# Moving two casts of q and k, and one batch's transposes, in the queues of a fused attention and mixer kernel

## The chip, the cores and the metric

The kernel runs on one core of a Trainium2 chip. A core has five engines that work side by side and keep in step through semaphores: TensorE (PE in the profile; its weight loads are PEld), VectorE (DVE), ScalarE (ACT), GpSimd (POOL) and SyncE (SP). Each takes its instructions in the order in which the program wrote them for that engine. Transfers between the chip's memory (DRAM here) and the on-chip buffers are issued by an engine and carried out by 16 DMA engines; this kernel issues them from SP and from POOL, and each of these two has its own DMA queue. An instruction that waits holds up everything behind it on its engine, a DMA that is to be issued too.

The metric is the time of one execution on the device in microseconds (us), the median of several runs.

## The reference

Eight batches, 8 heads, 576 tokens, head dimension 64. Attention with a causal mask and a bias made from a running sum of s; then a mixer on the attention's output with a low-rank product over the tokens and a two-layer product over the channels:

```python
scores = scale * np.matmul(q, k.transpose(0, 1, 3, 2))
cum = np.cumsum(np.maximum(s, 0.0), axis=-1)
bias = -(cum[:, :, :, None] - cum[:, :, None, :])
scores = np.where(causal, -1000000000.0, scores + np.minimum(bias, 0.0))
attn = softmax(scores)                      # exp(scores - max), divided by its sum
x = (attn @ v) with the heads side by side  # (8, 576, 512)
h = xt @ U @ V                              # xt: x with tokens last; U 576x32, V 32x576
u = x + h.transpose(0, 2, 1)
out = u + np.maximum(u @ w_ch1, 0.0) @ w_ch2   # 512 -> 2048 -> 512
```

Inputs and output are float32; the products run in bfloat16.

## The kernel before

**Groups.** The mixer works on pairs of batches, four groups of 1152 tokens. While TensorE runs the two layers of one group (`layer1`, line 551; `layer2`, line 570), the attention of the next two batches is mixed into the same instruction streams. The function `beside` does that: it takes both as generators whose steps name a cost, and decides by these costs which of the two writes its next instructions. [...]

**Attention of a batch** (`attention`, `scores`, `weigh`). For each head: four rounds of score products on TensorE (line 323), an exponential on ACT behind each (line 329), and behind the second exponential a causal select on POOL (line 344), which puts zeros above the diagonal. The head is weighed with v (line 373) one head later, between the second and the third round of the next head; the last head of a batch is weighed right behind its own scores. After each head, `attention` calls `at_head(h)`, where the program puts transfers and conversions for later batches.

**How q and k come in.** From batch 3 on, `cast(b)` (line 153) issues two DMAs from POOL that read k and q of a batch as float32 and write them as bfloat16 into the DRAM scratch `kq_rows`. `turn_batch(b)` (line 766) then issues from SP, for each of the batch's four pairs of heads, two transposing DMAs from `kq_rows` into kT and qT (`turn_kq`, line 174) and two small transfers of bias rows (`bias_rows`, line 281) that have to follow them: 16 DMAs. kT and qT have room for two batches. Batch 2 comes in otherwise, through `load_six` on POOL's queue and transposes on TensorE; only its bias rows are transfers of SP.

**How v comes in.** `fetch_v(b, t)` (line 194) is a DMA from SP of 128 tokens (the fifth tile has 64) as float32 into the buffer vf, which holds one batch. `cast_v(b, t)` (line 200) converts a tile on POOL into v_raw, from which `weigh` reads it. A fetch for batch b+1 has to wait for the conversions of batch b.

**The stretch around the change**, in the order of the program:

- `second()`: the weighing of batch 1's last heads beside the first layers; then on POOL two kinds of memset on v_raw (lines 806, 808), the five cast_v(2, t), and cast(3). SP has just issued the five fetch_v(2, t) and the bias rows of batch 2.
- between the two calls of `beside`: on SP an output transfer, the five fetch_v(3, t), then turn_batch(3).
- the attention of batch 2 (c == 2 in `ahead_of`): behind head 5 cast_v(3, 0); behind head 6 cast(4), then cast_v(3, 1) and cast_v(3, 2); behind head 7 cast_v(3, 3), cast_v(3, 4), and on SP fetch_v(4, t).
- the attention of batch 3: behind head 0 turn_batch(4) on SP.
- `mix(1)`: on DVE the sum of x and the low-rank part (line 522), on SP the transposes of x into uT (line 526), which `layer1` of the second group reads.

Of the kernel before, what the change touches and what calls it, by code (L numbers as in the profile page):

```python
# [41 lines left out]
def kernel(  # L42
# [110 lines left out]
    def cast(b):  # L153
        for i, src in enumerate((k, q)):
            nc.gpsimd.dma_start(
                out=kq[i, HP * b : HP * b + HP, :PAIR].rearrange("n (r c) -> r n c", r=128),
                in_=src[b]
                .rearrange("(n h) s d -> n (h s d)", h=2)
                .rearrange("n (r c) -> r n c", r=128),
            )  # L160
# [8 lines left out]
    def turn_kq(n):  # L169
        if not n < BH // 2:  # L170
            return
        for i, to in enumerate((kT, qT)):
            rows = kq[i, n]
            nc.sync.dma_start(
                out=to[n % RING][:, : 2 * S],
                in_=bass.AP(
                    tensor=rows.tensor, offset=rows.offset, ap=[[D, 2 * S], [1, 2 * D]]
                ),
                transpose=True,
            )  # L180
# [11 lines left out]
    def fetch_v(b, t):  # L192
        rows = slice(128 * t, min(128 * t + 128, S))
        nc.sync.dma_start(
            out=vf0[v_rows(t), t], in_=v[b, :, rows].rearrange("h p d -> p h d")
        )

    def cast_v(b, t, engine=None):
        n = v_rows(t)
        (engine or nc.gpsimd).tensor_copy(v_raw[b // 2 % 2][n, 5 * (b % 2) + t, :, :D], vf0[n, t])  # L200
# [76 lines left out]
    def bias_rows(n):  # L277
        if not n < BH // 2:
            return
        for to, r in ((kT, A_K), (qT, A_Q)):  # L280
            nc.sync.dma_start(out=to[n % RING][D:KA, : 2 * S], in_=aug_v[r, n])
# [79 lines left out]
    def weigh(b, h, p, scalar=False):  # L361
        bi = b % 2
        vr, x = v_raw[b // 2 % 2], x_sb[b // 2 % 2]
        diag = (D0, D1, D2, D3, D4)
        off = (O0, O1, O2, O3)
        pv = bank("pv", 2)
        pv3 = pv[:, : 5 * (D + 1)].rearrange("p (t e) -> p t e", e=D + 1)
        for it in range(5):
            for j in range(it + 1):
                at = diag[j] if j == it else off[j] + 128 * (it - j - 1)  # L370
                if it == 4 and bi == 1:
                    at -= 64
                nc.tensor.matmul(  # L373
                    pv3[:, it, :], lhsT=p[:, at : at + 128],
                    rhs=vr[:, 5 * bi + j, h, :],
                    start=(j == 0), stop=(j == it),
                )
        rec = work.tile([128, 5], FP32, tag="rec", name="rec")
        nc.vector.reciprocal(rec, pv3[:, :, D])  # L379
        n = 5 if bi == 0 else 4  # L380
        if scalar:
            for t in range(n):
                nc.scalar.mul(x[:, t, h * D : h * D + D], pv3[:, t, :D], rec[:, t : t + 1])
            return
        nc.vector.tensor_mul(  # L385
            x[:, 5 * bi : 5 * bi + n, h * D : h * D + D], pv3[:, :n, :D],
            rec[:, :n].unsqueeze(2).to_broadcast([128, n, D]),
        )
        if bi:
            (nc.scalar.mul if b == 1 and h < H - 1 else nc.vector.tensor_scalar_mul)(  # L390
                x[64:128, TAIL, h * D : h * D + D], pv3[64:128, 4, :D], rec[64:128, 4:5]
            )
# [149 lines left out]
    def layer1(cuts, by_block=False):  # L542
        jobs = [(c, nf) for c in cuts for nf in range(16)]
        if by_block:

            jobs.sort(key=lambda job: job[1] + 1.5 * (job[0] != cuts[0]))
        for (c0, c1), nf in jobs:
            cw = c1 - c0
            f1 = bank("f", 3)
            for kt in range(4):  # L550
                nc.tensor.matmul(  # L551
                    f1[:, :cw], lhsT=w1[:, kt, 128 * nf : 128 * nf + 128],
                    rhs=uT[:, kt, c0:c1],
                    start=(kt == 0), stop=(kt == 3),
                )
                if kt == 1:
                    yield 2 * cw / 2400.0
            nc.scalar.activation(hT[:, nf, c0:c1], f1[:, :cw], RELU)  # L558
            yield 2 * cw / 2400.0

    def layer2(g, tl):
        for t in tl:
            more = g == 0 and t < TAIL

            last = g == len(GROUPS) - 1 and t == 8
            for cs in (slice(0, 256), slice(256, 512)) if last else (slice(0, 512),):
                cw = cs.stop - cs.start
                f2 = bank("f", 3)
                for kt in range(16):
                    nc.tensor.matmul(  # L570
                        f2[:, :cw], lhsT=hT[:, kt, 128 * t : 128 * t + 128], rhs=w2[:, kt, cs],
                        start=(kt == 0), stop=(kt == 15 and not more),
                    )
                    if kt % 2 == 1:
                        yield 0.43
                if more:
                    nc.tensor.matmul(
                        f2, lhsT=V_cat[:, t, :], rhs=ux0, start=False, stop=True
                    )
                o = work.tile([128, d_model], FP32, tag="o", name="o", bufs=5)  # L580
                nc.vector.tensor_add(o[:, :cw], x_sb[g % 2][:, t, cs], f2[:, :cw])  # L581
                if t == TAIL:
                    for bi, b in enumerate(GROUPS[g]):
                        nc.sync.dma_start(
                            out=out[b, 512:576, :], in_=o[64 * bi : 64 * bi + 64, :]
                        )
                else:
                    r0 = 128 * (t if t < TAIL else t - 5)
                    nc.sync.dma_start(
                        out=out[GROUPS[g][t > TAIL], r0 : r0 + 128, cs], in_=o[:, :cw]  # L590
                    )
# [3 lines left out]
    def beside(back, ahead, ratio, lead):  # L595
        due, live = -lead * ratio, True
        for cost in back:
            due += cost * ratio
            while live and due > 0:
                spent = next(ahead, None)  # L600
                if spent is None:
                    live = False
                else:
                    due -= spent
        for _ in ahead:
            pass
# [159 lines left out]
    def turn_batch(b, p0=0, p1=HP):  # L766
        for n in range(HP * b + p0, HP * b + p1):
            turn_kq(n)
            if n > HP * b:
                bias_rows(n - 1)  # L770
        if p1 == HP:
            bias_rows(n)
# [27 lines left out]
    def second():  # L800
        yield from second_front
        for head in second_done:
            weigh(*head)
            yield 0.48
        yield 0.6
        nc.gpsimd.memset(v_raw[1][:, :, :, D : D + 1], 1.0)
        for i in (0, 1):
            nc.gpsimd.memset(v_raw[1][:64, 4 + 5 * i], 0.0)
        for t in range(5):
            cast_v(2, t)  # L810
        cast(3)
        yield from mix(0)

    def first_layer():
        yield from layer1(PARTS, by_block=True)
        yield from layer2(0, range(1))

    beside(first_layer(), second(), 15.8 / 17.3, 1.3)
    for t in range(5):
        fetch_v(3, t)  # L820
    turn_batch(3)

    def both_layers(g):
        if g == 0:
# [7 lines left out]
    def ahead_of(c):  # L832


        def at_head(h):

            if h == 0 and c == 3:
                turn_batch(c + 1)
            if h == 0 and c in (4, 6):
                cast(c + 1)  # L840
                turn_batch(c + 1, 0, 2)
                for t in range(5):
                    fetch_v(c + 1, t)
                turn_batch(c + 1, 2, HP)
            if h == 0 and c == 5:
                cast(c + 1)
                turn_batch(c + 1)
            if h == 6 and c == 2:
                cast(c + 2)
            if 5 <= h and c + 1 < B:  # L850
                for t in ((0,), (1, 2), (3, 4))[h - 5]:
                    cast_v(c + 1, t)
            if h == 7 and c in (2, 4):
                for t in range(5):
                    fetch_v(c + 2, t)

        return at_head
# [52 lines left out]
```

## Time and profile before

| what | us |
|---|---|
| median of 3 runs | 374.39 (374.31 to 374.79) |
| the profiled execution, its own time | 374.12 |
| its span, first to last instruction | 372.4 |
| TensorE busy | 360.5 |
| ACT busy | 212.3 |
| DVE busy | 139.1 |
| POOL busy | 108.3 |
| share of the 16 DMA engines' span in SP's queue | 45.6% |
| the same for POOL's queue | 27.7% |

How to read the rows. A row of the timeline has the start in us from the span's start, the duration, the engine (with a q for its sequencer, which issues DMAs), the line, the operation, what it writes and reads, the shape and the count of instructions that it stands for. In brackets stands how long the engine was idle just before, and what ended that. [...] A row of a DMA queue in a window gives packets, MB, and the time of the packets as a share of what 16 engines have in that window. An idle engine costs time only where the chain of work that ends last runs through it.

### The profile page before, as it was taken

What the parts mean: (1) busy time and instruction counts of PE and PEld (TensorE: products, weight loads), DVE (VectorE), ACT (ScalarE), POOL (GpSimd) and SP (SyncE); (2) the same over time, 40 slices, a digit from 0 to 9 for tenths busy, and PEclk for the clock granted to TensorE, in tenths of its full rate; (3) what the DMA queues carried; (4) which work ended last, traced back from release to release, by engine and by line L of the source; (5) the groups of instructions that cost most, each with busy time, mean ns of one, the idle gap of its engine ahead of it and who ended that gap; (6) DMA issues with size and microseconds to landing.
All of it is one profiled execution on the core that took longest, in us unless ns stands there. A gap on an engine that the chain in (4) does not pass through costs nothing.

```text
span 372.4 us, 8251 instructions
## 1 busy us (share of the span) xinstructions
PE 360.5 (97%) x3234; PEld 221.4 (59%) x3255; DVE 139.1 (37%) x310; ACT 212.3 (57%) x499; POOL 108.3 (29%) x166
## 2 busy tenths in 40 slices
PE   7899999999999989999999999999999999999996
PEld 3577684568776446666654446666654446565444
DVE  8878855652224551221243721212233710000221
ACT  6988982479897019889850009888840007772000
POOL 8895982312634103243150003242120000000000
PEclk9999999999999999999999999999999999999999
DMA  7999999798799869999995558892001550000122
GB/s 118 181 153 213 173 207 214 153 204 164 138 242 178 104 157 172 180 212 163 217 155 165 101 141 154 156 193 47 2 30 58 126 143 28 2 0 30 70 72 85
DMA packets 124039, 49.32 MB, mean 132 GB/s; under 512 B 104896, under 2 KB 119200, under 8 KB 124000
## 3 DMA queue, kind: packets, MB, share of 16 engines
q1 hardware_dynamic: 104374, 34.45, 45.6%
q0 software_dynamic: 19056, 14.22, 27.7%
q8 instruction: 25, 0.41, 0.5%
q10 hardware_dynamic: 570, 0.12, 0.2%
q14 instruction: 14, 0.11, 0.1%
HBM read 37.67 MB, written 15.79 MB: 144 GB/s over the span
## 4 chain that ended last, share of the span: by engine, by line
PE 87%; DVE 6%; ACT 3%; issue 1%; POOL 1%; DMA 1%; ACTq 0%; POOLq 0%; DVEq 0%
PE ps_f L551 32%; PE ps_f L570 31%; PE ps_s L323 11%; PE ps_pv L373 8%; DVE x_sb L522 2%; ACT pT L329 1%; PE ps_f L518 1%; PE ps_f L444 1%; PE ps_pv L296 1%; DVE qT L288 1%; DVE kT L288 1%; PE ps_s L315 1%; ACT x_sb L329 1%; DMA uT<-x_sb 1%; ACT hT L558 1%
## 5 line engine op out<-in xcount | busy, mean ns | idle before, releaser
L551 PE MATMUL ps_f<-uT,w 128*128 128x384 bf16 (+3 forms) x832 | 158.4, 313 | 0.9 <-DMA uT<-x_sb 0.9
L329 ACT ACTIVATE pT<-ps_s 128x448 bf16<-128x448 f32 x232 | 109.8, 526 | 60.4 <-PE ps_s L323 58.6
L570 PE MATMUL ps_f<-w,hT 128*128 128x512 bf16 (+1 forms) x571 | 136.8, 373 | 1.1
L558 ACT ACTIVATE hT<-ps_f 128x384 bf16<-128x384 f32 (+3 forms) x208 | 101.9, 492 | 46.8 <-PE ps_f L551 45.5
L551 PEld LDWEIGHTS <-w 128*128 128x128 bf16 x832 | 72.3, 98 | 34.0 <-issue 2.2
L570 PEld LDWEIGHTS <-hT 128*128 128x128 bf16 x592 | 54.9, 98 | 57.1 <-issue 3.9
L344 POOL TENSOR_SCALAR_AFFINE_SELECT pT<-pT 128x640 bf16<-128x640 bf16 x58 | 43.9, 756 | 150.5 <-ACT pT L329 150.0
L323 PE MATMUL ps_s<-qT,kT 68*128 68x128 bf16 (+9 forms) x576 | 80.8, 239 | 3.2 <-ACT pT L329 0.8
L323 PEld LDWEIGHTS <-kT 68*128 68x128 bf16 (+1 forms) x576 | 46.2, 97 | 29.9 <-issue 5.5
L379 DVE RECIPROCAL rec<-ps_pv 128x5 f32<-128x5 f32 x64 | 12.5, 195 | 120.2 <-PE ps_pv L373 119.9
L581 DVE TENSOR_TENSOR o<-x_sb,ps_f 128x512 f32<-128x512 bf16 (+1 forms) x37 | 24.9, 673 | 86.3 <-PE ps_f L570 85.6
L373 PEld LDWEIGHTS <-pT 128*128 128x128 bf16 x870 | 33.7, 97 | 8.7 <-ACT pT L329 1.0
L373 PE MATMUL ps_pv<-v_raw,pT 128*128 128x65 bf16 x870 | 36.7, 194 | 0.7 <-POOL pT L344 0.5
L385 DVE TENSOR_TENSOR x_sb<-ps_pv,rec 128x320 bf16<-128x320 f32 (+1 forms) x64 | 29.3, 458 | 2.3
L200 POOL CAST v_raw<-vf 128x512 bf16<-128x512 f32 (+1 forms) x35 | 21.3, 616 | 16.3 <-DMA vf<-in_v_dram 11.4
L522 DVE TENSOR_TENSOR x_sb<-x_sb,ps_f 128x512 bf16<-128x512 bf16 x32 | 21.2, 687 | 7.4 <-PE ps_f L518 7.1
L288 DVE COPY kT<-ps_pv 64x576 bf16<-64x576 bf16 x14 | 11.2, 803 | 3.5 <-ACT kT L288 2.8
L296 PEld LDWEIGHTS <-hT 96*128 96x128 bf16 x144 | 8.1, 97 | 4.4 <-DMA hT<-in_k_dram 1.1
L518 PE MATMUL ps_f<-ux_sb,V_cat 128*128 128x512 bf16 x27 | 10.2, 379 | 0.4
L288 DVE COPY qT<-ps_pv 64x576 bf16<-64x576 bf16 x12 | 9.6, 803 | 2.5 <-ACT qT L288 1.8
L315 PE MATMUL ps_s<-uT 128*128 128x512 bf16 (+2 forms) x21 | 7.6, 451 | 1.8 <-DVE uT L106 1.6
L288 ACT COPY kT<-ps_pv 64x576 bf16<-64x576 bf16 x4 | 3.2, 796 | 9.2 <-PE ps_pv L296 9.2
(109 smaller groups left out, 152.0 us busy)
## 6 DMA issues: line engine op xcount, KB each, us to landing
out_dram<-o SPq DMA_DIRECT2D x31, 256.0 KB
vf<-in_v_dram SPq DMA_DIRECT2D x28, 256.0 KB
w<-in_moe_w_ch_dram POOLq DMA_DIRECT2D x8, 512.0 KB, 9.4
kq_rows<-in_k_dram POOLq DMA_DIRECT2D x5, 576.0 KB, 7.0
kq_rows<-in_q_dram POOLq DMA_DIRECT2D x5, 576.0 KB, 10.0
out_dram<-o SPq DMA_DIRECT2D x10, 128.0 KB
hT<-in_k_dram POOLq DMA_DIRECT2D x4, 288.0 KB, 8.6
hT<-in_q_dram POOLq DMA_DIRECT2D x4, 288.0 KB, 10.6
```

The source lines that it names most:

```text
L200: (engine or nc.gpsimd).tensor_copy(v_raw[b // 2 % 2][n, 5 * (b % 2) + t, :, :D], vf0[n, t])
L288: one()
L323: nc.tensor.matmul(ps[:, col : col + w], lhsT=kt_[:rows, c + kc : c + kc + 128], rhs=qt_[:rows, c + qc : c + qc + w], start=True, stop=True,)
L329: nc.scalar.activation(p[:, at : at + w], ps[:, :w], EXP, scale=scale)
L344: nc.gpsimd.affine_select(out=diagonal, in_=diagonal, compare_op=ALU.is_ge, fill=0.0, base=0, pattern=[[0, 5], [1, 128]], channel_multipli ...
L373: nc.tensor.matmul(pv3[:, it, :], lhsT=p[:, at : at + 128], rhs=vr[:, 5 * bi + j, h, :], start=(j == 0), stop=(j == it),)
L385: nc.vector.tensor_mul(x[:, 5 * bi : 5 * bi + n, h * D : h * D + D], pv3[:, :n, :D], rec[:, :n].unsqueeze(2).to_broadcast([128, n, D]),)
L522: nc.vector.tensor_add(x[:, t, :], x[:, t, :], hp_)
L551: nc.tensor.matmul(f1[:, :cw], lhsT=w1[:, kt, 128 * nf : 128 * nf + 128], rhs=uT[:, kt, c0:c1], start=(kt == 0), stop=(kt == 3),)
L558: nc.scalar.activation(hT[:, nf, c0:c1], f1[:, :cw], RELU)
L570: nc.tensor.matmul(f2[:, :cw], lhsT=hT[:, kt, 128 * t : 128 * t + 128], rhs=w2[:, kt, cs], start=(kt == 0), stop=(kt == 15 and not more),)
L581: nc.vector.tensor_add(o[:, :cw], x_sb[g % 2][:, t, cs], f2[:, :cw])
```

## The change

Three moves; no instruction is added or removed.

1. In `second()`, cast(3) stands ahead of the five cast_v(2, t) on POOL instead of behind them.
2. On SP, turn_batch(3) stands ahead of the five fetch_v(3, t) instead of behind them.
3. In the attention of batch 2, cast(4) is issued behind head 4 instead of behind head 6.

```diff
@@ second() @@
         for i in (0, 1):
             nc.gpsimd.memset(v_raw[1][:64, 4 + 5 * i], 0.0)
+        cast(3)
         for t in range(5):
             cast_v(2, t)
-        cast(3)
         yield from mix(0)
...
     beside(first_layer(), second(), 15.8 / 17.3, 1.3)
+    turn_batch(3)
     for t in range(5):
         fetch_v(3, t)
-    turn_batch(3)
...
                 cast(c + 1)
                 turn_batch(c + 1)
-            if h == 6 and c == 2:
+            if h == 4 and c == 2:
                 cast(c + 2)
             if 5 <= h and c + 1 < B:
                 for t in ((0,), (1, 2), (3, 4))[h - 5]:
```

The functions that are moved, as they stand in both kernels:

```python
def cast(b):
    for i, src in enumerate((k, q)):
        nc.gpsimd.dma_start(out=kq[i, HP * b : HP * b + HP, :PAIR]..., in_=src[b]...)

def turn_batch(b, p0=0, p1=HP):
    for n in range(HP * b + p0, HP * b + p1):
        turn_kq(n)
        if n > HP * b:
            bias_rows(n - 1)
    if p1 == HP:
        bias_rows(n)
```

## The prediction

> **What bounds the kernel now.** I read the page's busy shares first, then TensorE's timeline for places where it stands, then the timelines of POOL and SP around those places, and last the packets that each DMA queue moved in chosen windows.
>
> ```profile
> PE 360.5 (97%) x3234; PEld 221.4 (59%) x3255; DVE 139.1 (37%) x310; ACT 212.3 (57%) x499; POOL 108.3 (29%) x166
> ```
>
> TensorE is busy 360.5 of 372.4 us, so the change can win only what TensorE stands idle for in its reach (from 57 to 137 us), and can lose whatever new wait it makes. Three rows of TensorE's timeline (start, duration, line, shape, count, and in brackets idle time and what ended it):
>
> ```profile
> 78.75 0.55 PE L323 MATMUL ps_s<-qT,kT 68*128 68x64 bf16 x6
> ...
> 99.88 0.64 PE L373 MATMUL ps_pv<-v_raw,pT 128*128 128x65 bf16 x15 [0.49 <-POOL pT L344]
> ...
> 137.19 0.48 PE L551 MATMUL ps_f<-uT,w 128*128 128x384 bf16 x2 [0.89 <-DMA uT<-x_sb]
> ```
>
> There are two stalls: 0.49 us before the last head of batch 2 is weighed (TensorE was ready at 99.39), where POOL's causal select came late, and 0.89 us before layer 1 of the second group, where SP's transposes of x came late. Together 1.38 us: the most the change can win. The first row is batch 2's first scores. Now POOL:
>
> ```profile
> 56.08 0.99 POOL L808 MEMSET v_raw<- 64x520 bf16 x2
> ...
> 67.55 0.62 POOL L200 CAST v_raw<-vf 64x512 bf16<-64x512 f32 x1 [0.23 <-DMA vf<-in_v_dram]
> 68.11 0.84 POOL L155 DMA_DIRECT2D kq_rows<-in_k_dram  x1
> ...
> 93.17 0.75 POOL L344 TENSOR_SCALAR_AFFINE_SELECT pT<-pT 128x640 bf16<-128x640 bf16 x1 [2.04 <-ACT pT L329]
> 93.88 0.61 POOL L200 CAST v_raw<-vf 128x512 bf16<-128x512 f32 x1
> 95.80 0.75 POOL L344 TENSOR_SCALAR_AFFINE_SELECT pT<-pT 128x640 bf16<-128x640 bf16 x1 [1.31 <-ACT pT L329]
> 96.50 0.74 POOL L155 DMA_DIRECT2D kq_rows<-in_k_dram  x1
> 97.22 0.74 POOL L155 DMA_DIRECT2D kq_rows<-in_q_dram  x1
> 97.95 1.18 POOL L200 CAST v_raw<-vf 128x512 bf16<-128x512 f32 x2
> 99.08 0.75 POOL L344 TENSOR_SCALAR_AFFINE_SELECT pT<-pT 128x640 bf16<-128x640 bf16 x1
> 99.77 1.29 POOL L200 CAST v_raw<-vf 128x512 bf16<-128x512 f32 x2
> ```
>
> The selects are those of heads 5, 6 and 7 of batch 2; head 4's ended 2.04 before 93.17, at 91.13. Between heads 6 and 7 stand both issues of cast(4) and two conversions of v. At the pace of the heads (93.17 to 95.80 is 2.63) the last select would start at 98.43; it starts at 99.08. Then SP, in its order, with DVE's row for x:
>
> ```profile
> 68.47 10.62 SPq L194 DMA_DIRECT2D vf<-in_v_dram  x5
> 79.27 1.84 SPq L174 DMA_TRANSPOSE kT<-kq_rows  x1
> ...
> 97.17 1.39 SPq L589 DMA_DIRECT2D out_dram<-o  x3
> 98.61 12.08 SPq L194 DMA_DIRECT2D vf<-in_v_dram  x5
> 110.86 2.19 SPq L174 DMA_TRANSPOSE kT<-kq_rows  x1
> ...
> 131.93 3.91 SPq L526 DMA_TRANSPOSE uT<-x_sb  x3
> ```
>
> ```profile
> 128.49 3.93 DVE L522 TENSOR_TENSOR x_sb<-x_sb,ps_f 128x512 bf16<-128x512 bf16 x6 [0.82 <-PE ps_f L518]
> ```
>
> SP runs behind: x's first tile is ready near 129.2, its transpose is issued at 131.93, because SP still issues batch 4's turn (begun at 110.86, after a fetch of 12.08).
>
> The third thing to see is what a cast does to SP's transfers. Packets by queue (q1 is SP's, q0 POOL's) in the windows 61 to 66 us, 73.5 to 77.5, 68.4 to 71.5, and 71.5 to 78, in this order (packets, MB, share of 16 engines):
>
> ```profile
> q1 hardware_dynamic: 4236, 1.06, 107.2%
> ...
> q0 software_dynamic: 576, 0.65, 93.0%
> q1 hardware_dynamic: 560, 0.14, 26.8%
> ...
> q1 hardware_dynamic: 1157, 0.52, 62.1%
> ...
> q1 hardware_dynamic: 715, 0.18, 20.3%
> ```
>
> Alone, SP's queue moves 847 packets a us (4236 in 5 us). Beside a cast it gets one packet for one of the cast's: 140 a us. SP's v packets have 256 bytes (1.18 MB in 4608 packets, 1024 a full tile), the cast's 1152 (1024 packets for k and q), so a cast of some 7 us nearly stops a fetch of v.
>
> **The change, part by part.** *cast(3) ahead of cast_v(2).* POOL is free at 57.07, so cast(3) is issued 11 us sooner. Its transfer then falls into fetch_v(2), which is under way in the whole window from 61 to 66 and whose last conversion starts at 67.55. The cast's 1024 packets at 144 a us take 7.1 us, in which SP's queue moves 995 packets, which alone it does in 1.2. So fetch_v(2) ends 5.9 us later, and with it cast_v(2) (its last from 67.55 to 73.5), batch 2's bias rows and the output transfer that stand behind it on SP. Nothing stalls: batch 2's first scores, which need the bias rows, are at 78.75, and its first weighing, which needs v, follows them. Without that cover the cost would be up to those 5.9 us.
>
> *turn_batch(3) ahead of fetch_v(3).* The turn takes the place at 68.47, now 74.4. cast(3) has landed by then. It runs beside no cast. A turn on a queue nearly empty:
>
> ```profile
> 182.18 1.47 SPq L174 DMA_TRANSPOSE kT<-kq_rows  x1
> ...
> 198.17 0.24 SPq L281 DMA_DIRECT2D qT<-aug_rows  x1
> ```
>
> 16.2 us; batch 3's own was 17.9 before (79.27 to 97.17, when SP goes on). I take 16.2, the row that starts as this one will: fetch_v(3) is issued from 90.6 instead of 68.47. Its consumers, cast_v(3), stand on POOL at 93.88, 97.95 and 99.77, with the selects of heads 6 and 7 queued behind the first three of them. The 20 us of cover that the fetch had are nearly gone.
>
> *cast(4) two heads sooner.* POOL issues it at 91.13, behind head 4's select. The two issues (0.74 each) fit into the 2.04 us idle before 93.17, so they cost nothing there, and they leave the place before head 7's select: worth the 0.49. But cast(4)'s transfer now meets fetch_v(3), issued 0.5 us before it.
>
> How far the fetch gets is the unknown. The nearest row is the old meeting: fetch issued at 68.47, cast at 68.11, and by 71.5, where the cast takes over, SP's queue had moved 1157 packets, 128 of them of the output: one tile of v. The new fetch has 0.9 us more of a start, so some 800 packets more: about 1850, the first tile and most of the second. Under the cast it gets 715 (71.5 to 78): 2560. The cast ends 9.9 us after its issue (78.0 less 68.11), at 101.0; the 510 packets missing of the third tile take 0.6 more; from a fetch's last packets to POOL's conversion I take 1.5 (66, the end of the window that they fill, to 67.55). So the third tile is there at 103.1. cast_v(3,2) takes 0.62, head 7's select 0.75: TensorE, ready at 99.39, waits until 104.5. That is 5.1 against 0.49 before: 4.6 lost. Bounds: if the fetch starts 1.5 sooner, no tile is caught (0.49 won); if 1.5 later, the first tile is caught too and the wait grows to 6.7.
>
> *What follows.* fetch_v(4) no longer meets a cast, and is issued from about 103, as POOL frees the tiles, until 106.5; turn_batch(4) starts 4 us sooner than 110.86 while TensorE runs 4.6 later, so SP waits for x at the mix and the 0.89 goes. If the turn were still late, that 0.89 stays.
>
> Sum: +4.6 - 0.9 = +3.7. The profiled execution took 374.12 (span 372.4 and 1.7 around it), 0.27 under the median, 374.39: I predict 378.0, with 376.8 to 379.0 as this case's own range.
>
> [...]
>
> **The rivals.** *The fetch gets ahead of the cast* (the other side). Place: SP at the end of turn_batch(3). It decides at about 89.5: with three tiles' packets moved before 94.5 (91.13 + 3.4) the third lands by 97.8 and head 7's select starts at 98.43. For it: a turn on a wholly empty queue may take under 16.2, and a cast that starts slowly leaves SP more room. Against: it needs 1.1 us less than the two rows give. Both old stalls go: 374.39 - 1.38 = 373.0.
>
> *The first tile is caught too.* If the turn takes 17.9, the fetch starts at 92.3 and is stopped with some 500 packets through; after the cast 1860 are missing to the third tile, 2.2 us, so it lands at 104.7 and head 6's select is late as well. TensorE goes on at 106.1: 6.7 - 0.49 - 0.89 = +5.3, 379.7.
>
> *TensorE slows after the stand.* Its idle time is 12 us in the whole run, so no row shows what a stand of 5 us does. It could drop the clock; if the next head then runs at half speed, its 2.6 us become 5.2: 380.6. [...]
>
> *A partial catch*, between 374 and 376.5: the third tile mostly through before the cast.
>
> **How the numbers follow.** The forecast 0.45; fetch ahead 0.22; first tile caught 0.16; slower clock 0.12; partial 0.05. Half of the chance rests on 1 us of SP's time, so the range takes in the fast case and most of the late tile: 372.9 to 379.8, with the slow clock and a few of the others left out. 0.2% of the time, 0.75 us, is what a measurement of this kernel can tell from no change. Faster 0.23 (fetch ahead, and a little), same 0.02, slower 0.75.
>
> **What would show it.** POOL's two issues of cast(3) at 57 and of cast(4) at 91.1; cast_v(2) ending near 74; the turn's first transpose on SP near 74.4, the first fetch of v after it near 90.6; cast_v(3,2) idle on POOL for a DMA until about 103, and one idle time of TensorE of about 5 us behind head 7's select; no idle time before layer 1 of the second group. The prediction is wrong if fetch_v(3) starts before 89.5 or its third tile lands before 98, and the first part is wrong if cast_v(2) still ends at 68, which would put the turn at 68.5 and the fetch at 85.

## The result, and the profile after

The changed kernel takes 380.0 us (median of 4 runs, 379.25 to 380.48) beside 374.37 us (374.31 to 374.79, 4 runs) for the kernel before: a ratio of 1.0146, interval 1.0129 to 1.0162. The forecast was 378.0 with a range up to 379.8. The direction was right; the size was too small, and the result lies outside the range. Ratios and their intervals, here and below, are of the fast runs of both kernels in one session, so they need not be the quotient of two medians (the kernel before came to 373.71, 373.82 and 374.08 in the later sessions).

The profiled execution took 380.48 us (span 378.7), 6.36 more than that of before. TensorE's waits of the changed kernel (us in total, times, longest) and its timeline where it stands:

```profile
PE ps_pv L373 <- POOL pT L344: 5.0, 1, 5.0
```

```profile
103.16 1.00 PE L373 MATMUL ps_pv<-v_raw,pT 128*128 128x65 bf16 x15 [5.04 <-POOL pT L344]
106.46 1.03 PE L373 MATMUL ps_pv<-v_raw,pT 128*128 128x65 bf16 x15
```

One stand of 5.04 us has taken the place of the 0.49, and no idle time before layer 1 of the second group is left. The two weighings last 1.00 and 1.03, where one lasted 0.64 in the kernel before: TensorE runs slowly after the stand. The same in windows of the changed kernel (window, its length, busy time and count of PE, PEld, DVE, ACT, POOL, then the granted clock, the share of the DMA engines, GB/s):

```profile
101.00:101.50 0.50, 0.00 (x0) 0.00 (x0) 0.00 (x0) 0.00 (x0) 0.00 (x0) 0.91 1.28 290
101.50:104.00 2.50, 0.84 (x16) 0.85 (x17) 0.00 (x0) 0.00 (x0) 1.87 (x3) 0.50 1.34 234
104.00:108.00 4.00, 4.00 (x32) 2.81 (x30) 1.12 (x4) 1.75 (x4) 2.50 (x4) 0.50 1.17 314
108.00:108.50 0.50, 0.50 (x5) 0.36 (x4) 0.25 (x1) 0.06 (x1) 0.00 (x0) 0.77 1.34 246
```

The clock falls to half at 101.4 (0.91 of the first window is a mean of 1 and 0.5), 3.3 us into the stand, which began at 98.12 (103.16 less 5.04). It comes back at 108.2, 5 us after TensorE has work again.

POOL's timeline of the changed kernel (here as on SP, the row of a DMA is its issue, not its transfer):

```profile
57.48 0.84 POOL L155 DMA_DIRECT2D kq_rows<-in_k_dram  x1
...
74.78 0.61 POOL L200 CAST v_raw<-vf 64x512 bf16<-64x512 f32 x1 [0.28 <-DMA vf<-in_v_dram]
...
91.55 0.73 POOL L155 DMA_DIRECT2D kq_rows<-in_k_dram  x1
...
101.79 0.61 POOL L200 CAST v_raw<-vf 128x512 bf16<-128x512 f32 x1 [7.40 <-DMA vf<-in_v_dram]
102.36 0.74 POOL L344 TENSOR_SCALAR_AFFINE_SELECT pT<-pT 128x640 bf16<-128x640 bf16 x1
...
104.20 0.62 POOL L200 CAST v_raw<-vf 128x512 bf16<-128x512 f32 x1 [0.54 <-DMA vf<-in_v_dram]
104.76 0.75 POOL L344 TENSOR_SCALAR_AFFINE_SELECT pT<-pT 128x640 bf16<-128x640 bf16 x1
```

POOL waits 7.40 us for the first tile of batch 3's v, and head 6's select (102.36) stands behind that conversion. Not the third tile and head 7's select (104.76), as the forecast had it. SP's timeline of the changed kernel:

```profile
75.56 1.35 SPq L174 DMA_TRANSPOSE kT<-kq_rows  x1
...
91.90 0.24 SPq L281 DMA_DIRECT2D qT<-aug_rows  x1
92.24 10.21 SPq L194 DMA_DIRECT2D vf<-in_v_dram  x5
...
111.04 1.83 SPq L174 DMA_TRANSPOSE kT<-kq_rows  x1
...
136.61 3.88 SPq L526 DMA_TRANSPOSE uT<-x_sb  x3
```

The turn runs from 75.56 to 92.14, and the fetch is issued at 92.24: 0.69 us behind cast(4), not 0.5 ahead of it. What the two queues moved in the changed kernel, from 93 to 95.4, from 96.5 to 100 and from 101 to 102 (packets, MB, share):

```profile
q0 software_dynamic: 284, 0.33, 99.2%
q1 hardware_dynamic: 1, 0.00, 0.0%
...
q0 software_dynamic: 496, 0.55, 91.1%
q1 hardware_dynamic: 566, 0.14, 29.4%
...
q1 hardware_dynamic: 1145, 0.29, 127.8%
```

For the first 2.4 us SP's queue moves one packet, though two fetches of v have been issued on it. Then it gets about one for each of the cast's, 162 a us; when the cast has ended it gets 1145 in one us. The first tile needs 1024, so it comes when the cast is through.

The sum, from the starts of the same instructions of ACT in both traces (times of the kernel before): the changed kernel is 0.46 late at 57 us already (its start-up, ahead of the change's reach), 7.40 at 101, and 6.34 from 138 to the end. Of the 6.94 gained in between, the stand is 5.04 - 0.49 = 4.55; the 2.39 left is the slow stretch after it. The 2.39 is thus a remainder; the pair of filled and unfilled kernels below measures the same thing another way. The 1.06 that come back at the mix are mainly the 0.89 stall that went.

### The profile page after: what moved, and what is told of

The parts are those of the page before. It is cut to its first block, busy times and chain, and to the rows that moved or that the text cites. A ratio compares the mean times of both kernels' runs of the same rounds, so it can differ in the third digit from the quotient of the medians.

```text
span 378.7 us, 8272 instructions
## 1 busy us (share of the span) xinstructions
PE 364.3 (96%) x3255; PEld 223.4 (59%) x3255; DVE 139.0 (37%) x310; ACT 212.5 (56%) x499; POOL 107.9 (28%) x166
## 4 chain that ended last, share of the span: by engine, by line
PE 85%; issue 3%; ACT 3%; DMA 3%; DVE 3%; POOL 2%; POOLq 0%; ACTq 0%; DVEq 0%
PE ps_f L570 32%; PE ps_f L551 32%; PE ps_s L323 9%; PE ps_pv L373 7%; DMA w<-in_moe_w_ch_dram 2%; ACT pT L329 2%; DVE x_sb L522 2%; PE ps_f L518 2%; POOL pT L344 1%; PE ps_f L444 1%; PE ps_pv L296 1%; POOL v_raw L200 1%; DMA kT<-parts 1%; PE ps_s L315 1%; ACT x_sb L329 1%
## 5 line engine op out<-in xcount | busy, mean ns | idle before, releaser
L570 PE MATMUL ps_f<-w,hT 128*128 128x512 bf16 (+1 forms) x592 | 140.4, 373 | 0.4
L373 PE MATMUL ps_pv<-v_raw,pT 128*128 128x65 bf16 x870 | 37.6, 195 | 5.2 <-POOL pT L344 5.0
L373 PEld LDWEIGHTS <-pT 128*128 128x128 bf16 x870 | 34.5, 99 | 13.6 <-POOL pT L344 5.5
```

The source lines that it names most:

```text
L373: nc.tensor.matmul(pv3[:, it, :], lhsT=p[:, at : at + 128], rhs=vr[:, 5 * bi + j, h, :], start=(j == 0), stop=(j == it),)
L570: nc.tensor.matmul(f2[:, :cw], lhsT=hT[:, kt, 128 * t : 128 * t + 128], rhs=w2[:, kt, cs], start=(kt == 0), stop=(kt == 15 and not more),)
```

## The experiments

Two theories at first; each expectation says what it takes from them, and some set a theory of their own (C, D, E) or a rival beside them. A: the loss is one meeting of two transfers (fetch_v(3) has lost its lead and is caught by a cast(4) that comes earlier), plus the slow clock behind the stand. B: one of the moves costs by itself, or the loss is in transfers that stand behind. All kernels compute the same as before; those that fill TensorE's idle time add products that nobody reads.

**The two moves around the meeting, each undone.** All else is as in the changed kernel.

```diff
# order of before on SP
-    turn_batch(3)
     for t in range(5):
         fetch_v(3, t)
+    turn_batch(3)
```

> The changed kernel with the middle move undone: the five fetches of batch 3's v again ahead of its turn on SP; both casts stay early. Theory A (the late fetch of v meets cast(4)'s transfer): the fetch is issued near 75.5, when no cast is under way, v is there before 84, cast(4) meets the second half of the turn instead, whose consumers are far off. Both old stalls (0.49 and 0.89) go: 373.0. Theory B (the new place of cast(4) costs by itself, on POOL or by slowing the turn): the time stays at 376 or above, with TensorE idle behind a select of batch 2 or before batch 3's scores.

```diff
# cast(4) back behind head 6
-            if h == 4 and c == 2:
+            if h == 6 and c == 2:
```

> The changed kernel with the third move undone: cast(4) again behind head 6, turn ahead of fetch. Theory A: the fetch, issued near 91.8, has some 6 us alone before cast(4)'s transfer starts near 98; its tiles arrive in time or nearly so; TensorE's idle time behind head 6's select is under 0.5 us, the 0.49 behind head 7's stays, the 0.89 before layer 1 goes: 373.5. Theory C (a fetch behind the turn is too late for the conversions, wherever the cast is): an idle time of 3 us or more stays behind head 6's or head 7's select: 377 or above.

Measured: 373.29 us (372.85 to 374.16), ratio 0.9982 (0.9967 to 0.9997), with SP's order of before; 373.54 (373.01 to 374.27), ratio 0.9991 (0.9977 to 1.0006), with the late cast. Either undo takes the whole loss away (SP's old order leaves 0.5 us of the stall before layer 1, the late cast the 0.5 us before head 7 is weighed). SP's timeline with its old order, and then with the late cast, whose POOL row follows:

```profile
75.08 4.13 SPq L194 DMA_DIRECT2D vf<-in_v_dram  x5
79.38 1.95 SPq L174 DMA_TRANSPOSE kT<-kq_rows  x1
...
104.38 0.24 SPq L281 DMA_DIRECT2D qT<-aug_rows  x1
```

```profile
92.15 3.87 SPq L194 DMA_DIRECT2D vf<-in_v_dram  x5
```

```profile
95.28 0.61 POOL L200 CAST v_raw<-vf 128x512 bf16<-128x512 f32 x1 [0.72 <-DMA vf<-in_v_dram]
...
97.13 0.73 POOL L155 DMA_DIRECT2D kq_rows<-in_k_dram  x1
```

With the late cast the fetch is issued at 92.15, as late as in the changed kernel, and POOL waits 0.72 for the first tile instead of 7.40; the five issues of the fetch take 3.87 us on SP instead of 10.21 (there the third and the fourth issue, at 93.33 and 97.99, take 4.61 and 3.42; what holds them is not shown). A fetch as late as this is therefore affordable by itself; beside a cast it is not. With SP's old order it is the turn that meets cast(4): it takes 25 us (79.38 to 104.6) and nobody waits for it.

**One head later.** If the meeting decides, cast(4) one head later should let more of the fetch through.

```diff
-            if h == 4 and c == 2:
+            if h == 5 and c == 2:
```

> The changed kernel with cast(4) behind head 5 instead of head 4: its transfer starts 2.8 us later, near 96.3. Theory A: the fetch, issued near 91.8, gets the first two tiles through and is caught in the third: no idle time behind head 6's select, 3.5 to 5 us behind head 7's, the clock halved after it; 378 to 380.5. Theory C: the idle time stays behind head 6's select, about 5 us, and the time at 380.

Measured: 377.63 us (10 runs, scattered from 373.62 to 381.29), ratio 1.0066 (1.0033 to 1.0099). POOL's and TensorE's timelines:

```profile
105.43 0.62 POOL L200 CAST v_raw<-vf 64x512 bf16<-64x512 f32 x1 [4.65 <-DMA vf<-in_v_dram]
```

```profile
106.92 0.64 PE L373 MATMUL ps_pv<-v_raw,pT 128*128 128x65 bf16 x15 [2.28 <-POOL pT L344]
```

Four tiles came through and the fifth was caught, so the stand moved to batch 3's first head and shrank to 2.28. The expectation had the third tile caught and 378 to 380.5 us; the mechanism held, the tile and the time were wrong.

The scatter goes with the half clock. The mean clock of a run is 0.999 to 1.0 in the three runs up to 375.25 us, 0.995 in the five from 376.75 to 378.83, and 0.991 in the two longest. The profiled execution, one of the five, has a spell of 3.41 us at half rate, which makes 0.995 of a run of 376 us; one of 6.82 us, as in the changed kernel's trace, makes 0.991.

**The stand filled.** Does the slow clock cost, or only go along? First on the changed kernel as it is:

```diff
             if pending is not None:
+                if b == 2 and h == 7:
+                    ps = bank("f", 3)
+                    for _ in range(23):
+                        nc.tensor.matmul(ps, lhsT=w1[:, 0, :128], rhs=w1[:, 0, :512], start=True, stop=True)
                 weigh(*pending)
```

> The changed kernel with 23 matmuls of 128x512 whose result nothing reads, put on TensorE right before the weighing of batch 2's head 6, where it stood 5.04 us; they take some 5 us at full clock. Theory D (of the loss some 2.4 us are TensorE at half clock after the stand): the granted clock stays 1.00, the stretch is as long as before, and the time is 377.6. Theory E (the rest of the loss is the refilling of the pipeline after the stand): 380 or, with the added work, up to 381, whatever the clock.

Measured: 379.16 (378.0 to 380.06), ratio 1.014 (1.0115 to 1.0165), against 377.6 by theory D (the half clock costs) and 380 to 381 by theory E. POOL's timeline of it:

```profile
91.08 0.73 POOL L155 DMA_DIRECT2D kq_rows<-in_k_dram  x1
...
94.16 0.61 POOL L200 CAST v_raw<-vf 128x512 bf16<-128x512 f32 x1 [0.24 <-DMA vf<-in_v_dram]
...
101.88 0.61 POOL L200 CAST v_raw<-vf 128x512 bf16<-128x512 f32 x1 [5.34 <-DMA vf<-in_v_dram]
...
103.64 0.75 POOL L344 TENSOR_SCALAR_AFFINE_SELECT pT<-pT 128x640 bf16<-128x640 bf16 x1
```

This execution doesn't settle it: the fetch was issued 0.04 us ahead of the cast this time, so one tile came through and the meeting was another one (the one of the forecast, with head 7's select ending at 104.4). And later it stood 1.46 us for v of batch 5, which the unfilled one didn't. So the meeting was fixed for a pair: two bias rows of SP are repeated ahead of the fetch, without and with 26 such products.

```diff
     turn_batch(3)
+    bias_rows(4 * 3 + 3)
     for t in range(5):
         fetch_v(3, t)
```

> The changed kernel with two bias rows of SP repeated between turn_batch(3) and fetch_v(3), so that the fetch is issued surely behind cast(4), at about 93 us. Theory A (the fetch is caught whole; of the loss some 5 us are TensorE's stand and some 2.4 the half clock after it): the first tile of v is converted at about 102, TensorE stands 5.0 to 5.6 behind head 6's select, the granted clock is at 0.5 for 6 to 7 us, alignment by 108 us about +7.2, time 380.2 to 381.0. Theory B (the half clock costs nothing; what follows the stand is lost to transfers that stand behind the fetch): the same time, but it stays when the stand is filled with work (next kernel).

> The same, and TensorE fills the stand with 26 products of 128x512 on weights (5.5 us of work whose result nobody reads) before head 6 is weighed. Theory A: no record under 0.9 of the clock, heads behind the stand at 0.62 and not 1.0 a weighing, the loss by 108 us 2 to 2.5 smaller than in the kernel before this one (about +5), time 378.0 to 378.6, or up to 1.5 more if batch 5's v comes late again, as with the 23 products. Theory B: the same 380.2 to 381.0 as without the filling.

Measured: 379.98 (379.46 to 381.03), ratio 1.0161 (1.0139 to 1.0183), without the filling; 379.02 (378.8 to 379.7), ratio 1.0135 (1.0118 to 1.0151), with it. The windows behind the stand, without and with it:

```profile
103.00:109.00 6.00, 5.56 (x47) 4.09 (x48) 1.38 (x4) 1.98 (x5) 3.44 (x6) 0.50 1.24 286
```

```profile
102.00:104.00 2.00, 2.00 (x26) 1.24 (x24) 0.17 (x1) 0.00 (x0) 1.47 (x3) 1.00 1.35 217
104.00:108.00 4.00, 4.00 (x46) 2.99 (x44) 1.20 (x4) 2.92 (x8) 2.19 (x4) 1.00 1.16 316
```

The filling keeps the clock full, so it is the stand that halves it. By the starts of the same instructions of ACT the loss grows, from the start-up until the clock is full again, by 7.20 without it (0.90 to 8.10) and by 5.29 with it (0.07 to 5.36). The filling overshoots by some 0.6 (it ends at 103.17; head 6's select had ended at 102.54), which makes the price of the half clock 1.9 + 0.6 = 2.5 in this pair, close to the 2.39 in the changed kernel. In the medians only 0.96 is left, less than the 2 to 2.5 expected: 0.6 is the overshoot, and 0.59 goes again after 165 us, where v of batch 5 is waited for. The time without the filling is a little under its expectation. The intervals of the two ratios overlap a little, so the pair shows the clock by its records, and its price by two traces rather than by the medians.

**The fetch ahead of the last pair of the turn.** The rival of the forecast ("the fetch gets ahead of the cast") made true by placing.

```diff
-    turn_batch(3)
+    turn_batch(3, 0, 3)
     for t in range(5):
         fetch_v(3, t)
+    turn_batch(3, 3, HP)
```

> The changed kernel, but the five fetch_v(3) stand ahead of the last of the four pairs of heads in turn_batch(3), not behind it. Theory A (only the order of fetch_v(3) and cast(4) in time costs): fetch_v(3) is issued from about 87.5, 3.5 us ahead of cast(4), and its first three tiles land before 97; no stand at heads 6 and 7 and none before layer 1: 373.0, ratio 0.996 to 0.998. Theory C (the fetch needs the whole lead of 20 us that it had, for instance since the transposes and bias rows ahead of it on SP's queue slow it): the third tile lands after 98 and time is 375 to 378.

Measured: 373.99 (373.2 to 376.05), ratio 1.0003 (0.9987 to 1.0019). SP's and POOL's timelines:

```profile
86.42 4.15 SPq L194 DMA_DIRECT2D vf<-in_v_dram  x5
```

```profile
97.09 1.17 POOL L200 CAST v_raw<-vf 128x512 bf16<-128x512 f32 x2
99.03 0.75 POOL L344 TENSOR_SCALAR_AFFINE_SELECT pT<-pT 128x640 bf16<-128x640 bf16 x1 [0.77 <-ACT pT L329]
```

POOL's three conversions ahead of head 7's select start without a wait for v, and both old stalls are gone: 5.3 us of lead over cast(4), which was issued at 91.68, were enough. The loss is gone as well; the gain of 1.4 is not there in the median, against the 373.0 expected. The fetch two pairs earlier:

```diff
-    turn_batch(3)
+    turn_batch(3, 0, 2)
     for t in range(5):
         fetch_v(3, t)
+    turn_batch(3, 2, HP)
```

> The changed kernel with the five fetch_v(3) between the second and the third pair of heads of turn_batch(3): fetch_v(3) issued at about 83, 8 us ahead of cast(4). Theory A: no stand at heads 6 and 7, none before layer 1, in every run: 372.8 to 373.4, ratio 0.996 to 0.998; the kernel with the fetch ahead of the last pair alone came to 373.99, with runs between 373.2 and 376.05, because its margin of some microseconds is used up in some runs. Rival (there is another wait that takes what the two stalls give, as v of batch 5 in group 2): 373.5 to 374.3 again, with the two stalls gone in the profile.

Measured: 373.41 (372.74 to 374.58), ratio 0.999 (0.9979 to 1.0001), between the two expectations. The profile shows neither stall. So the kernels that have neither stall (these two and the third part alone, below) come to between 1.0003 and 0.9989, not to the 0.9963 that 1.38 us would make. Yet their traces are shorter by about that much: from 57 us to the end, by the starts of the same instructions of ACT, this kernel gains 1.10, the one before it 1.37 and the third part alone 1.36 on the trace of the kernel before. The next experiments say more on this.

**Each part alone, and the change without its first part.**

```diff
# first part alone: from the kernel before
+        cast(3)
         for t in range(5):
             cast_v(2, t)
-        cast(3)
```

> The first part of the change alone: cast(3) ahead of cast_v(2). Theory A (it trades the place of cast(3) for that of fetch_v(2) and costs and wins nothing by itself): fetch_v(3) issued at 75 instead of 68.5, batch 3's turn from about 79.4 to 95.5, cast(4) at 96.5 as before; both stalls of before still there (0.4 to 0.9 each), 373.7 to 374.4, ratio 0.999 to 1.001. Rival (the early cast is what shortened the queue in the two kernels that lost the stall before layer 1): that stall goes and the time is 373.2 to 373.5.

```diff
# second part alone: from the kernel before
+    turn_batch(3)
     for t in range(5):
         fetch_v(3, t)
-    turn_batch(3)
```

> The second part alone: turn_batch(3) ahead of fetch_v(3), cast(3) late and cast(4) behind head 6 as before. Theory A (the fetch must be through before a cast starts; without the early cast(3) the turn starts at 76.2 and the fetch at 92.9 to 94, a cast's packets start 1.5 us behind its issue, at 98 to 98.6): tiles one to three land in time for heads 6 and 7, the last 500 to 1500 packets are caught, the fifth tile lands between 104 and 108, and TensorE stands 1 to 3.5 us at batch 3's head 0, perhaps with a spell of half clock behind it: 374.5 to 378. Rival (the swap is harmless as long as cast(4) stands behind head 6, as with the early cast(3) at 373.5): 373.3 to 374.

```diff
# third part alone: from the kernel before
-            if h == 6 and c == 2:
+            if h == 4 and c == 2:
```

> The third part alone: cast(4) behind head 4, SP's order as before. Theory A (the cast hurts only a fetch that it meets; it meets the last pairs of batch 3's turn, which nobody needs before head 4 of batch 3): head 7's select on time, the stall before layer 1 smaller or as before: 373.3 to 374.0, ratio 0.998 to 1.000. Rival (an early cast(4) costs in itself, by the turn that it slows): the turn ends after 106, fetch_v(4) and turn_batch(4) come later than before and the stall before layer 1 grows over 0.9: 374.4 to 375.

```diff
# second and third part: from the changed kernel
-        cast(3)
         for t in range(5):
             cast_v(2, t)
+        cast(3)
```

> The change without its first part: cast(3) behind the five cast_v(2) again. Theory A (the first part only changes who waits for whom ahead of the turn: fetch_v(2) is done sooner, but the turn then waits for cast(3)): first transpose of batch 3 between 75 and 77, fetch_v(3) issued at 92 to 93.5, behind cast(4), a stand of 5 to 6 and 380 to 381. Rival (the early cast(3) is what made the turn late): the turn starts at 69 to 73, fetch_v(3) is issued ahead of 89.5 and the time is 373.0 to 373.5.

Each ratio is to the kernel before in the same session.

| parts done | median, us | ratio to before, interval | longest wait of TensorE on POOL's select |
|---|---|---|---|
| first | 373.76 | 1.0005 (0.9996 to 1.0015) | 0.5 |
| second | 376.35 | 1.0055 (1.0035 to 1.0075) | 1.7 |
| third | 373.42 | 0.9989 (0.9977 to 1.0001) | none |
| first and second | 373.54 | 0.9991 (0.9977 to 1.0006) | 0.5 |
| first and third | 373.29 | 0.9982 (0.9967 to 0.9997) | none |
| second and third | 381.07 | 1.0188 (1.0168 to 1.0209) | 5.4 |
| all three | 380.0 | 1.0146 (1.0129 to 1.0162) | 5.0 |

The first and the third part alone cost nothing. The second alone costs 0.55%, unless the first stands with it; so theory B holds in part for this one move.

The first part alone met neither of its expectations: its time is that of the kernel before, but its profile has no stall before layer 1, and from 57 us to the end it gains 1.05 on the trace of the kernel before. That stall is in none of these profiles but one (0.53, first and third part), though only the kernel before has it at 0.89. So the profiled execution of the kernel before seems not to be typical in this place, and most of the 0.89 was probably not there to be won in its other executions, which were not profiled. SP's timeline of the second part alone, and TensorE's:

```profile
69.94 0.37 SPq L589 DMA_DIRECT2D out_dram<-o  x1
76.25 1.35 SPq L174 DMA_TRANSPOSE kT<-kq_rows  x1
...
95.22 0.24 SPq L281 DMA_DIRECT2D qT<-aug_rows  x1
95.56 3.92 SPq L194 DMA_DIRECT2D vf<-in_v_dram  x5
```

```profile
100.13 0.63 PE L373 MATMUL ps_pv<-v_raw,pT 128*128 128x65 bf16 x15 [1.70 <-POOL pT L344]
103.42 0.64 PE L373 MATMUL ps_pv<-v_raw,pT 128*128 128x65 bf16 x15 [1.37 <-POOL pT L344]
```

SP waits from 70.3 to 76.25 for cast(3), which POOL issues at 70.27 in this execution:

```profile
70.27 0.84 POOL L155 DMA_DIRECT2D kq_rows<-in_k_dram  x1
```

The fetch comes 3.4 us later than with the early cast (95.56 for 92.15), and no cast has to meet it to make it late for head 6. The second stand, of 1.37, is POOL's own queue: behind head 6's select stand both issues of cast(4) and two conversions, and head 7's select follows them at 102.61 without a wait for a transfer. Theory A had the right time here (374.5 to 378) by a wrong course: it had the last tiles caught by cast(4) and a stand in batch 3. With the early cast left out of the whole change, the fetch is issued at 95.17, later than the 92 to 93.5 expected, and the ratio is 1.0188 instead of 1.0146: the first part is what makes the swap bearable, and saves 0.4% of the time in the changed kernel.

The lowest ratio is that of the first and third part without the second: 373.29, 0.18% (0.03 to 0.33%) faster than the kernel before. It is the lowest of thirteen kernels, and the interval of the third part alone overlaps it, so that it is the best is not shown.

## Why the prediction was wrong, point by point

Two steps failed. The course of the meeting was wrong: *cast(4) two heads sooner* let 1850 packets of the fetch through ahead of the cast, and none got through. And the sum left out a term: TensorE at half clock behind the stand, 2.39 us, stood among the rivals and not in the sum. By size, this second step is what carries the result out of the range, since the stand itself came to the size in the sum.

- *What bounds the kernel*: right as to place, too generous as to prize. TensorE was the bound, and both stalls went where the forecast said. But the kernels without either stall gain at most 0.11% by their ratios, not 1.38 us (0.37%). One profiled execution shows a stall of that execution; that the 0.89 goes from the trace with the first part alone, at a ratio of 1.0005, speaks against its being in every run of the kernel before, but this was not measured, and stays open.
- *cast(3) ahead of cast_v(2)*: right. POOL issues it at 57.48, cast_v(2) ends at 75.4 for the 74.1 of the forecast, nothing stalls, and alone it costs nothing (1.0005). The last conversion starts 1.3 later than said, 0.46 of it start-up.
- *turn_batch(3) ahead of fetch_v(3)*: the course right, the place off by 1.6 us. First transpose at 75.56 for 74.4; turn 16.6 for 16.2; fetch at 92.24 for 90.6. This lies at the "1.5 later" of the forecast's own bound. cast(4) was 0.42 later than said too (91.55 for 91.13), but the rest turned the order of the two transfers round: the fetch behind cast(4), not ahead.
- *cast(4) two heads sooner*: the step of the course that failed. It had 1850 packets through before the cast, taken from the old meeting of fetch and cast. In the changed kernel SP's queue moved 1 packet from 93 to 95.4. Two things were wrong: the 1.6 us of the step before, and the old meeting as a measure. There the cast's packets began late, by this row of the kernel before for 68.5 to 70.9 us (no other row of POOL's queue but these 2 packets, 2.7 us after the issue):

```profile
q0 software_dynamic: 2, 0.00, 1.3%
q1 hardware_dynamic: 893, 0.45, 68.1%
```

  Here SP's queue had nothing left to move, and the cast's packets began 1.4 us after its issue, at 93.0; from 91.6 to 92.9 SP's queue had only this, the turn's last rows, and POOL's nothing:

```profile
q1 hardware_dynamic: 15, 0.02, 6.4%
```

  The filled kernel, where the fetch went 0.04 ahead, had head 7's select end at 104.4, against 104.5 in the forecast: the course was the right one for that order. But by 93.6 only 1034 packets, one tile, had got through, not 1850, so the close agreement of the end is partly luck.
- *The size of the stand*: 5.04 for 5.1, an agreement by chance. It is another head's stand, from another tile. The rival "the first tile is caught too" put it at 6.7, since it let TensorE wait for the third tile as well. But TensorE had work between the two weighings (103.16 to 106.46, at half clock), and head 7's select had ended at 105.51.
- *TensorE slows after the stand*: it was a rival of 0.12, and should have been a term of the sum. It measured 2.39 (2.6 forecast for it, with half speed as an assumption; the granted clock was 0.50). The two rivals were priced each by itself; they came together, as in all three traces with a stand of about 5 us that nothing filled (4.89, 5.04 and 5.38 us). The traces' sum is 4.55 + 2.39 - 1.06 = 5.88, and with the start-up of 0.46 it is 6.34, beside 6.36 between the two profiled executions. Without the 2.39, the first sum would be 3.49, near the 3.7 of the forecast. The medians differ by 5.63.
- *What follows*: the term was right, the 0.89 went (1.06 by the traces), but not in the way that was said. turn_batch(4) did not start 4 us sooner: it started at 111.04, and fetch_v(4) was issued from 104.24 to 110.87. And the stall is gone as well in the first part alone, where fetch_v(4) takes 12.76 us beside cast(4), as before. So what took it away in the changed kernel is not shown.

## What to carry to other kernels

Before a transfer gives up its lead, look for what is issued on the other queue close to its new place: here the fetch lost nothing when it was issued 5.0 or 5.3 us ahead of the cast (ratios 0.9991 and 1.0003), 0.66% at 3.6 us ahead, and 1.46% at 0.69 us behind. The first and the third move cost nothing singly (1.0005 and 0.9989), the second 0.55%, and with the first ahead of it nothing (0.9991); all three made 1.46% together. Where a change makes TensorE stand for some us, put the half clock behind the stand into the sum (2.1 to 2.8 us for a stand of 4.9 to 5.4 here) and not into a rival. And take a stall seen in one profiled execution as the most it can be worth: here 1.38 us of stalls gave no more than 0.4 us by the ratios where both went.

## What the runs showed of the hardware

**A transfer issued while the other queue was busy could begin late, up to 4.1 us after its issue.** With nothing on POOL's queue, a fetch issued at 92.15 (the late cast) moved 8 packets until 93.2, none of them of v, and 2819 from 93.3 to 96.3:

```profile
q1 hardware_dynamic: 8, 0.01, 2.6%
...
q1 hardware_dynamic: 2819, 0.71, 117.7%
```

By the starts of the packets, its first came 1.07 us after its issue, as in the three other traces in which no packet of POOL's queue moved then. Beside a cast that had just begun, one issued at 92.24 moved its first packets at 95.7, 3.5 us after its issue (4.1 in the two kernels with the repeated bias rows). It went the other way round as well. Of the 70 casts of the fourteen traces, the 18 that found SP's queue at rest (under 20 packets until their start) had their first packets 1.43 to 1.45 us after their issue, the other 52 from 1.44 to 3.88 us after it. The longest is in the kernel with the fetch ahead of the last pair: cast(4) was issued at 91.68, and from 91.7 to 95.3 this was the only row of the two queues:

```profile
q1 hardware_dynamic: 1773, 0.45, 134.1%
```

From 93.8 to 95.0 only 28 of these packets moved, so it was not simply the packets of the other queue that kept the cast out. And being first did not keep the place. In the filled kernel (23 products) the fetch was moving from 92.1 on and the cast began at 93.2; from 93.5 to 95.9 the two queues moved:

```profile
q0 software_dynamic: 362, 0.42, 112.2%
q1 hardware_dynamic: 26, 0.01, 1.1%
```

So in this meeting the cast that began pressed a moving fetch far back for more than 2 us (with cast(4) behind head 5 the fetch got 149 packets beside 326 from 97.1 to 99.5). In the changed kernel the two queues shared about packet by packet from 96.5 to 100 (496 of the cast's, 566 of SP's), after 284 and 1 from 93 to 95.4. It was not so with every cast: after cast(3) of the changed kernel had begun near 59.9, SP's queue moved 966 packets (0.13 MB) from 60 to 62.4, beside 403 of POOL's. Why is not settled by these runs.

**The half clock behind a stand lasted 3.4 or 6.8 us, and the shortest stand with one was 2.28 us.** From 101.41 to 108.23 it was half in the changed kernel, 6.8 us. In the kernel with cast(4) behind head 5 the stand was 2.28 us and the clock fell only after work had begun again (106.92), from 107.41 to 110.82, 3.4 us (the ends from the means 0.91 and 0.68):

```profile
107.00:107.50 0.50, 0.50 (x16) 0.50 (x17) 0.00 (x0) 0.00 (x0) 0.50 (x1) 0.91 1.26 287
107.50:110.50 3.00, 3.00 (x19) 1.98 (x17) 0.91 (x3) 1.44 (x4) 0.07 (x1) 0.50 1.15 229
110.50:111.00 0.50, 0.50 (x5) 0.37 (x4) 0.00 (x0) 0.50 (x2) 0.00 (x0) 0.68 0.89 168
```

Two stands of 1.70 and 1.37 us, 3.3 us apart, left it full in the profiled execution of the second part alone (two of its ten runs have a mean clock of 0.995). In the other two traces with such a spell the stands were 4.89 and 5.38 us, and the spell lasted 6.8 us again: 102.55 to 109.38 in the unfilled kernel with the repeated bias rows, 101.17 to 108.0 without the early cast (the ends from the means 0.55, 0.62 and 0.67 of windows of 0.5 us). What sets these lengths is not shown.

In the three traces with 6.8 us the spell began 0.9 to 2.2 us before the stand ended (1.75 in the changed kernel, 101.41 to 103.16), and the rest of it fell on work: TensorE worked 5.07 us at half clock in the changed kernel, 5.94 in the unfilled kernel with the repeated bias rows and 4.59 without the early cast, and the sums of the traces leave 2.39, 2.80 and 2.14 for it, a little under half each time.
